# A rewritten head: load order, fold steps ahead of attention, and two batches hosted phase by phase

## The chip, the cores and the metric

The kernel runs on one core of a Trainium2 chip. The metric is the device time of one execution in microseconds (us), as the median of several runs. The engines named here are PE (matrix multiplications and transposes), ACT (exp and copies), DVE (products, reciprocals and copies), POOL (casts of loaded data) and SP (whose queue issues the loads). The program gives each engine its own list of instructions, and in the profile each works through its list in that order.

## What is computed

Eight batches of sparse causal attention, eight heads each, then a feed-forward network with a product in place of an activation:

```python
scores = scale * np.matmul(q, k.transpose(0, 1, 3, 2))       # 8 x 8 heads, 576 x 576, head size 64
mask_local = (rel >= 0) & (rel < stride)                      # heads 0 to 3
mask_strided = (rel >= 0) & (pos[None, :] % stride == pos[:, None] % stride)   # heads 4 to 7
...
x = np.ascontiguousarray(attn_out.transpose(0, 2, 1, 3)).reshape(B * S, H * D)   # 4608 x 512
a = x @ w1
b = x @ w2
h = a * b @ w3
return (h @ w_out).astype(np.float32)
```

The inner width d_ff is 1024. The kernel computes in fp16 with fp32 sums.

## The kernel before

**Tiling.** Since there is nothing between w3 and w_out, the kernel first forms their product w34 (the *fold*): eight blocks `jc`, each with eight transposes of w3 (`fold_tr`, tile `trp`, evacuated by one DVE and then one ACT copy into `w3T`) and eight matmuls in two halves (`fold_mm`, tile `ops`). The network then runs over nine tiles of 512 tokens. A tile has 24 *halves*, each of four 128x512 matmuls: sixteen of `ab_halves` (a: x by w1, copied out by ACT into `asb`; b: x by w2, multiplied with `asb` on DVE into `abt`) and eight of `o_halves` (o: `abt` by w34, copied out by ACT and stored).

**Attention** is done by pairs of heads, four pairs per batch, two local and then two strided. They are called P0 to P31 here; P0 to P3 are batch 0, P4 to P7 batch 1. The phases of a pair are:
- T: transposes of q and k into the PSUM tile `pt` (L224; for the first pair of a batch also those of the rest of the rows, L232), copied to `qT` and `kT` by ACT, or by ACT and DVE;
- S: scores (L266), into the tile `sps` and for the last columns into `pt`; then exp on ACT in two pieces (L286, `pte`) and the product with the mask on DVE (L287, `ptm`);
- PV: probabilities by v (L308), written into `sps` again, for strided pairs with a second part into the tile `pm`; then reciprocal and product on DVE (`rcp`, `xqs`, L312 and L313);
- T2: transposes back (L320), into the same buffer as `pm`, copied into `xT`, the input of the network.

There is one buffer each for `sps` (pool psA), for `pt` (psT) and for `pm` and T2 (psM). `ph_TS(s, t)` emits S of one pair and T of the next in one `pt` tile.

**Order.** All of PE's work is kept in the order in which it is written. A list `stream` holds the phases of all pairs with GAP marks between them (L407 to L447), and `host` emits the halves of a fold or a tile and, after each, the phases up to the next gaps, so that a tile's gaps are spread evenly over its halves. `batch_end[b]` is the place in the stream up to which a batch must be done before the next tile, because a tile needs the xT of its batch. Before, fold halves host batch 0; then the first nine or ten halves of tile 0 run without attention (`lead=9`), and the other halves of tile 0 host batch 1. From tile 1 on, tile t hosts batch t+1.

**Loads.** All loads are issued from SP's queue in written order, into nine staging buffers (`stg`), and cast to fp16, by POOL except for w1's four column blocks, which ACT casts. The order before is in the calls in front of the fold.

Of the kernel before, what the change touches and what calls it, by code (L numbers as in the profile page):

```python
# [19 lines left out]
def kernel(  # L20
# [12 lines left out]
    B, H, S, D = q.shape  # L33
# [7 lines left out]
    KF = DF // P  # L41
# [25 lines left out]
    AHEAD = 2  # L67

    def pe(ins):
        return tc.keep_in_program_order(ins)  # L70

    def copy(eng, out, in_):
        if eng == "a":
            nc.scalar.copy(out=out, in_=in_)  # L74
        elif eng == "v":
            nc.vector.tensor_copy(out=out, in_=in_)  # L76
        else:
            nc.gpsimd.tensor_copy(out=out, in_=in_)  # L78
# [47 lines left out]
    w1h = consts.tile([P, KM, DF], FP16)  # L126
    w2h = consts.tile([P, KM, DF], FP16)
# [9 lines left out]
    def load_wo(g, eng):  # L137
        src = moe_w_out.rearrange("(c p) n -> p c n", p=P)
        st = stgp.tile([P, 2, DM], FP32, tag="stg")
        nc.sync.dma_start(st, src[:, 2 * g:2 * g + 2, :])  # L140
        copy(eng, woh[:, 2 * g:2 * g + 2, :], st)

    def load_w3(jc, eng):
        st = stgp.tile([P, DF], FP32, tag="stg")
        nc.sync.dma_start(st, moe_w3[bass.ds(jc * P, P), :])
        t = ffn.tile([P, DF], FP16, tag="w3n", bufs=4)
        w3n[jc] = t
        copy(eng, t, st)

    def load_w12(g):  # L150
        cs = bass.ds(g * 256, 256)
        for wd, wh, eng in ((moe_w1, w1h, "a"), (moe_w2, w2h, "p")):
            st = stgp.tile([P, KM, 256], FP32, tag="stg")
            nc.sync.dma_start(st, wd.rearrange("(c p) n -> p c n", p=P)[:, :, cs])
            copy(eng, wh[:, :, cs], st)
# [4 lines left out]
    def load_qk(b, grp, engs="pp"):  # L160
        for nm, ten, eng in (("q", q, engs[0]), ("k", k, engs[1])):
            st = stgp.tile([P, 4, 4, D], FP32, tag="stg")
            nc.sync.dma_start(st.rearrange("p h c d -> p h (c d)"),
                              ten[b, 4 * grp:4 * grp + 4, 0:NM].rearrange("h (p c) d -> p h (c d)", c=4))
            t = qkp.tile([P, 4, 4, D], FP16, tag=f"{nm}{grp}")
            copy(eng, t, st.rearrange("p h c d -> p c h d"))
            x16[(b, nm, grp)] = t
# [20 lines left out]
    def load_vS(b):  # L188
        vt = v16S[b % 2]
        for hp in range(2):  # L190
            st = stgp.tile([SQ, 2, ST, D], FP32, tag="stg")
            sf = st.rearrange("p h c d -> p h (c d)")
            sv = v[b, 4 + 2 * hp:6 + 2 * hp].rearrange("h (p c) d -> p h (c d)", c=ST)
            nc.sync.dma_start(sf[0:64], sv[0:64])
            nc.sync.dma_start(sf[64:SQ], sv[64:SQ])
            nc.gpsimd.tensor_copy(out=vt[:, 2 * hp:2 * hp + 2, :, 0:D], in_=st)  # L196
# [5 lines left out]
    pairs = []  # L202
# [130 lines left out]
    def ab_halves(tch):  # L333
        tok = bass.ds(tch * NT, NT)
        res = []

        def first():
            abts[tch] = ffn.tile([P, KF, NT], FP16, tag="abt", bufs=4, name=f"abt{tch}")

        for jc in range(KF):  # L340
            st = {}

            def a(jc=jc, st=st):
                if jc == 0:
                    first()
                aps = psF.tile([P, NT], FP32, tag="f")
                for ci in range(KM):
                    pe(nc.tensor.matmul(aps, w1h[:, ci, bass.ds(jc * P, P)], xT[ci][:, tok],  # L348
                                        start=(ci == 0), stop=(ci == KM - 1)))
                asb = ffn.tile([P, NT], FP32, tag="asb")  # L350
                nc.scalar.copy(out=asb, in_=aps)  # L351
                st["asb"] = asb

            def bb(jc=jc, st=st):
                bps = psF.tile([P, NT], FP32, tag="f")
                for ci in range(KM):
                    pe(nc.tensor.matmul(bps, w2h[:, ci, bass.ds(jc * P, P)], xT[ci][:, tok],  # L357
                                        start=(ci == 0), stop=(ci == KM - 1)))
                nc.vector.tensor_mul(abts[tch][:, jc, :], bps, st["asb"])  # L359

            res += [a, bb]
        return res

    def acc_halves(lhs, rhs, done):
        st = {}

        def half(hf):
            if hf == 0:
                st["ps"] = psF.tile([P, NT], FP32, tag="f", name="ops")
            for ci in range(4 * hf, 4 * hf + 4):  # L370
                pe(nc.tensor.matmul(st["ps"], lhs(ci), rhs(ci), start=(ci == 0), stop=(ci == KF - 1)))  # L371
            if hf == 1:
                done(st["ps"])

        return [lambda: half(0), lambda: half(1)]

    def o_halves(tch):
        res = []
        for ts in range(NT // P):
            def done(ps, ts=ts):  # L380
                osb = ffn.tile([P, DM], FP32, tag="osb", bufs=3)
                nc.scalar.copy(out=osb, in_=ps)  # L382
                nc.scalar.dma_start(out_r[tch * (NT // P) + ts], osb)

            res += acc_halves(lambda ci, ts=ts: abts[tch][:, ci, bass.ds(ts * P, P)],
                              lambda ci: w34[:, ci, :], done)
        return res

    def fold_tr(jc):
        js = bass.ds(jc * P, P)  # L390
        ps = psF.tile([P, 1024], FP16, tag="f", name="trp")
        for kc in range(KF):
            pe(nc.tensor.transpose(ps[:, kc * P:(kc + 1) * P], w3n[jc][:, bass.ds(kc * P, P)], id16))
        pv = ps.rearrange("x (c j) -> x c j", j=P)
        nc.vector.tensor_copy(out=w3T[0][:, :, js], in_=pv[:, 0:4, :])
        nc.scalar.copy(out=w3T[1][:, :, js], in_=pv[:, 4:8, :])
# [10 lines left out]
    stream = []  # L407
    batch_end = {}

    def add(f, *a):  # L410
        stream.append(lambda: f(*a))

    GAP = object()

    def gaps(n):
        stream.extend([GAP] * n)
# [10 lines left out]

    for p, s in enumerate(pairs):
        b, i = divmod(p, 4)
        if i == 0 and b < AHEAD:  # L430
            add(ph_TS, None, s)
            gaps(2)
        t = pairs[p + 1] if p + 1 < len(pairs) else None
        if i == 3 and (b + 1 < AHEAD or b + 1 == B):
            t = None
        add(ph_TS, s, t)
        gaps(2)
        if i or b >= AHEAD:
            add(ph_T2, pairs[p - 1])
            if i == 0:  # L440
                batch_end[b - 1] = len(stream)
        gaps(1)
        add(ph_PV, s)
        gaps(3)
        if i == 3 and (b + 1 < AHEAD or b == B - 1):
            add(ph_T2, s)
            batch_end[b] = len(stream)  # L447
    pos = [0]

    def host(units, upto, lead=0):  # L450
        n = len(units) - lead
        total = sum(x is GAP for x in stream[pos[0]:upto])
        done = 0
        for i, u in enumerate(units):
            u()
            if i + 1 == len(units):
                tgt = total + 1
            else:
                tgt = (total * max(i + 1 - lead, 0)) // n
            while pos[0] < upto and done < tgt:  # L460
                x = stream[pos[0]]
                pos[0] += 1
                if x is GAP:
                    done += 1
                else:
                    x()
# [2 lines left out]
    load_w3(0, "p")  # L469
    for g in range(4):  # L470
        load_wo(g, "p")
    load_w3(1, "p")
    load_qk(0, 0)
    load_rest(0)
    load_w3(2, "p")
    load_vL(0)
    load_w3(3, "p")
    load_qk(0, 1)
    load_w3(4, "p")
    load_w3(5, "p")  # L480
    load_vS(0)
    load_w3(6, "p")
    load_w3(7, "p")
    load_w12(0)
    load_w12(1)
    load_w12(2)
    load_qk(1, 0)
    load_rest(1)
    load_w12(3)
    load_vL(1)  # L490
    load_qk(1, 1)
    load_vS(1)
# [1 line left out]
    fold = []  # L494
    fold_tr(0)
    for jc in range(KF):
        h0, h1 = fold_mm(jc)
        fold.append(h0)
        if jc + 1 < KF:
            fold.append(lambda jc=jc: fold_tr(jc + 1))  # L500
        fold.append(h1)
    host(fold, batch_end[0], lead=3)
    load_qk(2, 0)
    load_rest(2)
    load_vL(2)
    host(ab_halves(0), pos[0] + 11, lead=9)
    load_qk(2, 1)
    load_vS(2)
    host(o_halves(0), batch_end[1])
    for tch in range(1, NTILE):  # L510
        units = ab_halves(tch) + o_halves(tch)
        if tch + 1 < B:
# [45 lines left out]
```

## Time and profile before

| | us |
|---|---|
| median of three runs | 295.56 |
| lowest and highest | 294.17 and 297.71 |
| the profiled execution | 296.77 |
| its span, first to last instruction | 295.1 |
| PE busy / ACT / DVE / POOL in the span | 264.6 / 150.2 / 148.4 / 104.6 |
| S of P0, P1, P2, P3 | 23.74, 29.32, 34.93, 41.44 |
| first a of tile 0 | 48.0 |
| T of P4, S of P4 | 58.39, 60.88 |
| S of P5, P6, P7 | 66.26, 70.75, 76.40 |
| first a of tile 1 | 84.31 |

The times in the lower part are starts in the profiled execution, in us from the start of the span. A busy PE is not a PE at its peak: at full clock a half of four matmuls takes 0.86 us start to start, at the low granted clock 1.7 us. In the rows of the timeline the first number is the start, the second the time from the start to the end of the group, then engine, line, operation, output and input, the number of instructions, and in brackets the idle time of the engine before it with what ended it. "PEclk" or "granted clock" is the share of the TensorE clock that was granted.

### The profile page before, as it was taken

To read this page: it belongs to the slowest core of one execution; us is meant where nothing else is said; L and a number is where in the kernel's file an instruction comes from. 1 tells how busy PE (TensorE), PEld (TensorE's weight loads), DVE (VectorE), ACT (ScalarE), POOL (GpSimd) and SP (SyncE) were. 2 spreads that over 40 slices of the span, in tenths; PEclk is the share of its full clock that TensorE was granted. 3 is DMA by queue.
4 is the path that set the end of the run, shared out by engine and by line. 5 is a ranking of instruction groups with operands and counts; after the bars stand their busy time and mean duration, and the time that the engine had idled before them with its cause. 6 is when DMAs were issued, how large, how long until landed. Compare 5 with 4: busy or idle time off the path is not lost.

```text
span 295.1 us, 6686 instructions
## 1 busy us (share of the span) xinstructions
PE 264.6 (90%) x2689; PEld 135.8 (46%) x2689; DVE 148.4 (50%) x279; ACT 150.2 (51%) x309; POOL 104.6 (35%) x118
## 2 busy tenths in 40 slices
PE   2468987997779999999999999999999999999995
PEld 1133543444445554555455455545554554444442
DVE  2016563474556774765558567646654663330420
ACT  2025784467545556556565655555555655323332
POOL 5649644565445833557566424110000000000000
PEclk9988997999959999999999999999999999999999
DMA  7999999996879957997989892120011002103003
GB/s 247 346 219 344 302 347 264 216 265 122 270 233 224 253 106 206 264 180 243 259 172 286 177 273 49 36 109 3 0 73 74 0 2 107 38 0 138 4 3 142
DMA packets 58656, 48.68 MB, mean 165 GB/s; under 512 B 29184, under 2 KB 49664, under 8 KB 58624
## 3 DMA queue, kind: packets, MB, share of 16 engines
q1 hardware_dynamic: 53440, 38.81, 53.9%
q10 hardware_dynamic: 5184, 9.44, 8.9%
q8 instruction: 21, 0.34, 0.5%
q14 instruction: 11, 0.09, 0.1%
HBM read 38.80 MB, written 9.44 MB: 163 GB/s over the span
## 4 chain that ended last, share of the span: by engine, by line
PE 71%; ACT 10%; DMA 8%; DVE 5%; issue 3%; POOL 1%; SPq 1%
PE bps L357 21%; PE aps L348 20%; PE ops L371 17%; ACT pte L286 4%; PE sps L308 4%; DMA st<-in_moe_w_dram 3%; DMA st<-in_moe_w_out_dram 3%; PE sps L266 2%; DVE ptm L287 2%; PE ps L320 2%; ACT osb L382 2%; PE pt L224 2%; DVE xqs L313 1%; DMA out_dram<-osb 1%; PE pt L266 1%
## 5 line engine op out<-in xcount | busy, mean ns | idle before, releaser
L348 PE MATMUL aps<-xT,w1h 128*128 128x512 f16 x288 | 77.0, 386 | 3.6 <-ACT xT L327 3.6
L351 ACT COPY asb<-aps 128x512 f32<-128x512 f32 x72 | 43.0, 597 | 67.0 <-PE aps L348 65.3
L357 PE MATMUL bps<-xT,w2h 128*128 128x512 f16 x288 | 75.7, 386 | 0.0
L359 DVE TENSOR_TENSOR abt<-bps,asb 128x512 f16<-128x512 f32 x72 | 49.6, 689 | 50.1 <-PE bps L357 48.0
L371 PE MATMUL ops<-w,abt 128*128 128x512 f16 x288 | 68.5, 379 | 0.0
L78 POOL CAST t<-st 128x1024 f16<-128x1024 f32 (+1 forms) x48 | 48.2, 1011 | 32.7 <-DMA st<-in_k_dram 14.5
L357 PEld LDWEIGHTS <-w2h 128*128 128x128 f16 x288 | 26.9, 99 | 35.0 <-issue 7.7
L286 ACT ACTIVATE pte<-sps 128x960 f16<-128x960 f32 (+1 forms) x32 | 31.7, 990 | 19.1 <-PE sps L266 18.0
L348 PEld LDWEIGHTS <-w1h 128*128 128x128 f16 x288 | 26.7, 100 | 28.7 <-issue 1.9
L371 PEld LDWEIGHTS <-abt 128*128 128x128 f16 x288 | 25.9, 98 | 27.7
L185 POOL CAST v16L<-st 32x768 f16<-32x768 f32 (+1 forms) x32 | 27.9, 872 | 22.0 <-PE aps L348 7.6
L382 ACT COPY osb<-ops 128x512 f32<-128x512 f32 x36 | 21.5, 598 | 25.8 <-PE ops L371 25.8
L313 DVE TENSOR_TENSOR xqs<-sps,rcp 96x768 f16<-96x768 f32 (+1 forms) x32 | 32.6, 1018 | 0.7
L287 DVE TENSOR_TENSOR ptm<-pte,maskL 128x1152 f16<-128x1152 f16 x16 | 13.6, 852 | 28.7 <-ACT pte L286 28.7
L287 DVE TENSOR_TENSOR ptm<-pte,maskS 72x1152 f16<-72x1152 f16 x16 | 14.8, 928 | 25.6 <-ACT pte L286 25.6
L74 ACT COPY qT<-pt 128x256 f16<-128x256 f16 (+2 forms) x64 | 23.3, 410 | 7.7 <-PE pt L232 4.5
L196 POOL CAST v16S<-st 72x1024 f16<-72x1024 f32 x16 | 17.8, 1116 | 21.5 <-PE pm L308 11.6
L308 PEld LDWEIGHTS <-ptm 72*128 72x128 f16 (+1 forms) x448 | 18.2, 98 | 14.7 <-DVE ptm L287 7.1
L371 PE MATMUL ops<-woh,w3T 128*128 128x512 f16 x64 | 19.6, 438 | 2.1 <-POOL woh L78 1.2
L266 PEld LDWEIGHTS <-kT 64*128 64x128 f16 x448 | 10.1, 97 | 16.2 <-issue 10.6
L320 PEld LDWEIGHTS <-xqs 72*128 72x128 f16 (+1 forms) x224 | 12.0, 99 | 8.1 <-DVE xqs L313 1.6
L76 DVE COPY kT<-pt 128x128 f16<-128x128 f16 (+1 forms) x28 | 11.5, 435 | 7.5 <-ACT qT L74 7.5
(53 smaller groups left out, 201.1 us busy)
## 6 DMA issues: line engine op xcount, KB each, us to landing
out_dram<-osb ACTq DMA_DIRECT2D x36, 256.0 KB, 2.0
st<-in_moe_w_dram SPq DMA_DIRECT2D x16, 512.0 KB, 8.7
st<-in_q_dram SPq DMA_DIRECT2D x16, 512.0 KB, 5.3
st<-in_k_dram SPq DMA_DIRECT2D x16, 512.0 KB, 6.3
st<-in_v_dram SPq DMA_DIRECT2D x32, 144.0 KB, 7.1
st<-in_v_dram SPq DMA_DIRECT2D x16, 256.0 KB, 7.4
st<-in_moe_w_out_dram SPq DMA_DIRECT2D x4, 512.0 KB, 8.1
st<-in_q_dram SPq DMA_DIRECT2D x8, 128.0 KB, 7.8
```

The costliest lines, as they stand in the source:

```text
L78: nc.gpsimd.tensor_copy(out=out, in_=in_)
L185: nc.gpsimd.tensor_copy(out=vt[pr, hs, :, 0:D], in_=st[pr])
L286: nc.scalar.activation(out=pte[0:kr, lo:hi], in_=src, func=AF.Exp, bias=0.0, scale=scale)
L287: nc.vector.tensor_mul(ptm[0:kr, 0:2 * S].rearrange("p (a x) -> p a x", x=w), pte[0:kr].rearrange("p (a x) -> p a x", x=w), _ap(mk, 0, [[m ...
L308: pe(nc.tensor.matmul(xps[:, h, i * 65:i * 65 + 65], s.ptm[0:kr, c0:c0 + P], vt[0:kr, 2 * (s.hp % 2) + h, c, :], start=True, stop=True))
L313: nc.vector.tensor_mul(s.xqs[0:w, cs[0]:cs[0] + l].rearrange("p i h d -> p h i d"), xv[:, :, :, 0:D], _ap(rcp, 0, [[rcp.ap[0][0], w], [ST, ...
L348: pe(nc.tensor.matmul(aps, w1h[:, ci, bass.ds(jc * P, P)], xT[ci][:, tok], start=(ci == 0), stop=(ci == KM - 1)))
L351: nc.scalar.copy(out=asb, in_=aps)
L357: pe(nc.tensor.matmul(bps, w2h[:, ci, bass.ds(jc * P, P)], xT[ci][:, tok], start=(ci == 0), stop=(ci == KM - 1)))
L359: nc.vector.tensor_mul(abts[tch][:, jc, :], bps, st["asb"])
L371: pe(nc.tensor.matmul(st["ps"], lhs(ci), rhs(ci), start=(ci == 0), stop=(ci == KF - 1)))
L382: nc.scalar.copy(out=osb, in_=ps)
```

## The change

There are four edits.
1. w1's blocks are cast by POOL, as w2's.
2. The loads in front of the fold are reordered: w3's blocks 2 and 3 come ahead of batch 0's q and k, and w1 and w2's fourth block ahead of batch 1's first.
3. The stream: T of a batch's first pair is a phase of its own for batches 0 to 2; T of the second local pair's successor (P2 and P6) is split off into a phase of its own (`late`); T2 stands after one gap in place of two; batch 1 ends within its own tile, as batch 0 does.
4. Batches 0 and 1 are placed by hand: `run(units, plan)` reads a text in which "u" emits the next unit and a digit that many phases. The fold of blocks 0 to 2 runs ahead of the first T. All sixteen halves of a and b of tile 0 run without attention, and batch 1 lies among the eight o halves. `host` loses its `lead`.

```diff
-        for wd, wh, eng in ((moe_w1, w1h, "a"), (moe_w2, w2h, "p")):
+        for wd, wh, eng in ((moe_w1, w1h, "p"), (moe_w2, w2h, "p")):
...
         b, i = divmod(p, 4)
-        if i == 0 and b < AHEAD:
+        last = i == 3 and (b < AHEAD or b == B - 1)
+        if i == 0 and b <= AHEAD:
             add(ph_TS, None, s)
-            gaps(2)
+            gaps(1)
         t = pairs[p + 1] if p + 1 < len(pairs) else None
-        if i == 3 and (b + 1 < AHEAD or b + 1 == B):
+        late = b < AHEAD and i == 1
+        if late or (i == 3 and (b < AHEAD or b + 1 == B)):
             t = None
         add(ph_TS, s, t)
-        gaps(2)
-        if i or b >= AHEAD:
+        gaps(1)
+        if i or b > AHEAD:
             add(ph_T2, pairs[p - 1])
             if i == 0:
+                gaps(1)
                 batch_end[b - 1] = len(stream)
-        gaps(1)
+        if late:
+            add(ph_TS, None, pairs[p + 1])
+        gaps(1 if i == 0 and b > AHEAD else 2)
         add(ph_PV, s)
         gaps(3)
-        if i == 3 and (b + 1 < AHEAD or b == B - 1):
+        if last:
             add(ph_T2, s)
             batch_end[b] = len(stream)
...
+    def run(units, plan):
+        it = iter(units)
+        for ch in plan:
+            if ch == "u":
+                next(it)()
+            elif ch != " ":
+                step(int(ch))
...
-    load_w3(1, "p")
+    for jc in range(1, 4):
+        load_w3(jc, "p")
     load_qk(0, 0)
     load_rest(0)
-    load_w3(2, "p")
+    load_w3(4, "p")
     load_vL(0)
-    load_w3(3, "p")
     load_qk(0, 1)
-    load_w3(4, "p")
     load_w3(5, "p")
+    load_w3(6, "p")
     load_vS(0)
-    load_w3(6, "p")
     load_w3(7, "p")
     load_w12(0)
     load_w12(1)
     load_w12(2)
+    load_w12(3)
     load_qk(1, 0)
     load_rest(1)
-    load_w12(3)
...
-        fold.append(h0)
-        if jc + 1 < KF:
-            fold.append(lambda jc=jc: fold_tr(jc + 1))
-        fold.append(h1)
-    host(fold, batch_end[0], lead=3)
+        tr = [lambda jc=jc: fold_tr(jc + 1)] if jc + 1 < KF else []
+        fold += [h0] + tr + [h1] if jc < 4 else [h0, h1] + tr
+    run(fold, "uuuuuuuuu 1 uu 1 uu 1 u 3 u 1 u 1 uu 1 u 1 uu 1 u 1 u 2")
...
-    host(ab_halves(0), pos[0] + 11, lead=9)
+    for u in ab_halves(0):
+        u()
     load_qk(2, 1)
...
-    host(o_halves(0), batch_end[1])
+    run(o_halves(0), "u 1 u 1 uu 1 u 4 u 2 u 2 u 3")
```

On the engines this gives the following sequences on PE (halves a, b and o as above, tr the fold's transposes). Batch 1 before: T a b S T a b a PV b o S T o T2 PV o S T o T2 PV o o S T T2 o PV o, then S and T of the next pairs, T2, and tile 1. Batch 1 after: T o S T o o PV o S T2 T PV o S T T2 o PV S o T2 PV T2, and tile 1, which opens with a, T of P8, b, S of P8.

More of the change, by code (lines that the diff above doesn't have):

```diff
@@ L448, with step, host @@
     pos = [0]
-    def host(units, upto, lead=0):
-        n = len(units) - lead
+    def step(n):
+        while n:
+            x = stream[pos[0]]
+            pos[0] += 1
+            if x is not GAP:
+                x()
+                n -= 1
+    def run(units, plan):
[5 more added lines that the diff above has]
+                step(int(ch))
+        assert next(it, None) is None
+    def host(units, upto):
+        n = len(units)
         total = sum(x is GAP for x in stream[pos[0]:upto])
@@ L455, in host @@
             u()
[L456 to L459, printed above, removed]
+            tgt = total + 1 if i + 1 == n else total * (i + 1) // n
             while pos[0] < upto and done < tgt:
@@ L497 @@
         h0, h1 = fold_mm(jc)
-        fold.append(h0)
-        if jc + 1 < KF:
-            fold.append(lambda jc=jc: fold_tr(jc + 1))
-        fold.append(h1)
-    host(fold, batch_end[0], lead=3)
+        tr = [lambda jc=jc: fold_tr(jc + 1)] if jc + 1 < KF else []
+        fold += [h0] + tr + [h1] if jc < 4 else [h0, h1] + tr
+    run(fold, "uuuuuuuuu 1 uu 1 uu 1 u 3 u 1 u 1 uu 1 u 1 uu 1 u 1 u 2")
+    assert pos[0] == batch_end[0]
     load_qk(2, 0)
@@ L505 @@
     load_vL(2)
-    host(ab_halves(0), pos[0] + 11, lead=9)
+    for u in ab_halves(0):
+        u()
     load_qk(2, 1)
     load_vS(2)
-    host(o_halves(0), batch_end[1])
+    run(o_halves(0), "u 1 u 1 uu 1 u 4 u 2 u 2 u 3")
+    assert pos[0] == batch_end[1]
     for tch in range(1, NTILE):
```

## The prediction, made before the changed kernel had run

> **What bounds the kernel now.** First the page, for shares and the forty slices.
>
> ```profile
> PE 264.6 (90%) x2689; PEld 135.8 (46%) x2689; DVE 148.4 (50%) x279; ACT 150.2 (51%) x309; POOL 104.6 (35%) x118
> PE   2468987997779999999999999999999999999995
> DMA  7999999996879957997989892120011002103003
> ```
>
> Past slice 12 (89 us) PE shows 9 in every slice until the tail, so nothing but PE time counts there. What can change lies in the first 89 us. There DMA is full for the first 57 us and PE is not, so I cut the head into the 3.41 us steps in which the granted clock changes. Columns: busy us of PE, granted clock, DMA share, GB/s.
>
> ```profile
> 17.22:20.63 3.41, 1.00 (x26) 1.00 1.33 174
> 20.63:24.05 3.42, 2.98 (x22) 0.50 1.04 313
> 44.53:47.94 3.41, 1.76 (x27) 1.00 1.20 260
> 47.94:51.35 3.41, 3.41 (x15) 0.50 1.13 256
> 71.83:75.25 3.42, 2.13 (x29) 1.00 0.69 134
> 78.66:82.07 3.41, 1.52 (x20) 1.00 0.48 162
> 82.07:85.49 3.42, 2.67 (x39) 0.50 0.76 214
> 85.49:88.90 3.41, 3.41 (x19) 0.50 1.10 308
> ```
>
> After a step in which PE was busy for 1.76 us or less, the next step runs at half clock; after 2.13 us it does not. A low step full of matmuls loses up to 1.7 us.
>
> Then the timeline, for what the attention waits for. One turn of it, pair P5 to P6:
>
> ```profile
> 66.43 0.39 PE L266 MATMUL sps<-qT,kT 64*128 64x96 f16 x10
> 66.86 0.97 ACT L286 ACTIVATE pte<-sps 128x960 f16<-128x960 f32 x1 [2.00 <-PE sps L266]
> 67.72 0.33 ACT L286 ACTIVATE pte<-pt 128x192 f16<-128x192 f32 x1
> 68.08 0.76 DVE L287 TENSOR_TENSOR ptm<-pte,maskL 128x1152 f16<-128x1152 f16 x1 [1.11 <-ACT pte L286]
> 68.90 0.54 PE L308 MATMUL sps<-v16L,ptm 128*128 128x65 f16 x12 [0.58 <-DVE ptm L287]
> 69.74 0.95 DVE L313 TENSOR_TENSOR xqs<-sps,rcp 96x768 f16<-96x768 f32 x1
> 70.75 0.40 PE L266 MATMUL sps<-qT,kT 64*128 64x72 f16 x14 [0.31 <-DVE xqs L313]
> ```
>
> PV writes into the score tile and there is one such tile, so the next S waits until xqs is read out: S to S was 4.5 us (66.26 to 70.75) with PE idle inside. Other turns took 5.4 to 6.5 us because halves or copies stood in the way. A turn holds about 2 us of attention on PE, so it needs some three halves of 0.86 us to fill it. Last, the ends of the tiles and the port hit:
>
> ```profile
> PE aps L348 <- ACT xT L327: 3.6, 6, 0.7
> 36.97 1.04 POOL L78 CAST t<-st 128x1024 f16<-128x1024 f32 x1 [0.30 <-DMA st<-in_moe_w_dram]
> 37.00 1.61 DVE L287 TENSOR_TENSOR ptm<-pte,maskS 72x1152 f16<-72x1152 f16 x1 [1.14 <-ACT pte L286]
> ```
>
> A mask product beside a POOL cast took 1.61 us, alone 0.76.
>
> **Part 1: loads, fold, batch 0.** No matmul, DMA or byte is added or removed. Two more w3 loads of 0.5 MB go ahead of q and k; such loads land 1.34 to 1.54 us apart (casts at 10.95, 12.29, 13.83), so q, k and rest come 2.9 us later and the cast of rest goes from 18.25 to 21.15. T of P0 ends at 21.8 and its copies, as in 18.92 to 21.12, at 24.0. Ahead of S0 the changed instruction order has one o half and the fold transposes of w3 block 4, whose cast follows rest by 1.7 us and takes 1.04 (23.9); transposes at the low clock take 1.0 us. So S0 is at 24.7, against 23.74. The fold steps done earlier (two halves and two sets of transposes, about 3 us) come out of DMA waiting and cost nothing, but the turns that they leave are not bound by PE. Turn by turn, in the changed order of ACT and DVE:
> - P0: ACT's copy of the fold stands ahead of exp (to 25.8), exp 1.2, mask 1.32 beside the v casts as in the row at 25.56, a v copy of 0.33 to 1.05 now between mask and PV, PV 0.54, xqs 1.2: S1 at 30.8 (6.1; before 5.57).
> - P1: T of P2 is a phase by itself now and needs the one pt tile, which exp of P1 reads until 1.95 after S1; then fold transposes, PV, xqs: 4.9, S2 at 35.7 (before 5.61).
> - P2: two halves, transposes and T2 stand ahead of PV; its second part waits for ACT's xT copy, queued behind exp, four copies of P3's T and two of the fold: 6.8, S3 at 42.5 (before 6.5).
> - P3: fold copy on ACT ahead of exp (0.9 late), then as before less the w1 cast of 0.93 that stood between its two exps: T2 at 48.6, against 47.70.
> Term: +0.9. Bounds: if every turn took its least (S0 23.9, then 4.5, 4.5, 5.0 and 5.3, the last from 41.43 to 47.70 less the cast), T2 at 43.2, -4.5; if the w1 casts, now POOL's (four of 1.04 us, beside w2's), hit the last mask, +0.6 more. I take +0.9, since the copies that I count stand in the order in every turn. SP's queue: w12's fourth column block passes q, k and rest of batch 1, so it comes at about 50 in place of 55; nobody needs it before half 13 (59). Batch 1's loads come 3 us later, with their use 6 us later.
>
> **Part 2: tile 0 and batch 1.** Before, ten halves ran bare from 48.0, then T of P4 at 58.39, and fourteen halves lay among the four pairs. Now sixteen and one run bare: 48.0 + 1.7 (low clock) + 17 x 0.864 = 64.4 for T of P4, and seven halves (6.0 us) are left for four turns. PE's work in them, 6.0 and 7.2 of attention (four S of 0.45, three T and four T2 of 0.43, PVs of 0.55 and 0.65), is far under their length. By rows: T to S 2.5 (58.39 to 60.88), 66.9; two turns of 4.5, 75.9; a strided one of 4.75 (exp 1.3, mask 0.76, PV 0.6, xqs 1.4, S 0.45, hand-overs 0.25), 80.6; last S to T2's end 5.5 (41.43 to 47.70 less the cast, plus 0.1), 86.1. Before, T2 of P7 ended at 84.3, with S of P8 and T of P9 done. Now tile 1's first a waits for xT (0.7), runs cold (to 87.3), T of P8 0.8, b 1.7 (89.8), and S of P8 waits: its four copies alternate between ACT and DVE on one tile (0.6, 0.68, 0.45, 0.42), and abt's product (0.69, ready only after b) stands ahead of the last on DVE: 91.0. S and T 0.8, PV 0.55: 92.35. The same work was done at 88.73 before. Term: +3.6. Turns shorter than 4.5, which no row shows, would be needed to take from it; POOL hits and the xT wait (row 70.75 to 76.41: 5.66) would add up to 2.
>
> Low steps: PE's share in 64.4 to 86.1 is 13.2 / 21.7, or 2.1 us per step, nearest to the 2.13 that kept the clock. I take 0 and keep +3.4 (two steps) and, were the end warm, -1.7.
> The Trainium skill, page "TensorE: Matmul & The Clock Gate", section "HAM oscillation — how this bites in real kernels", gives as its rule that only PE idle gaps over some 3.4 us matter. The rows differ: the longest gap in 44.53:47.94 was 1.5 us (before the PV at 45.46), and the next step was low. By the page the +3.4 cannot come, and the rival that needs it, below, would keep 0.05.
>
> **Part 3: T2 one unit earlier.** The changed order shows it inside every batch: S, T, b, T2, a, b, PV. At the tile ends it is unchanged from tile 2 on (S, T, o, T2, a), as the last unit takes all that is left. So the 3.6 us of waits stay. At the end of tile 1 it is worse: 27 gaps for 24 halves put S, T and T2 all behind the last o. xT, queued behind exp and qT, comes 3.25 after S; PE has 1.7 of work: wait 1.5, against 0.84 before (113.99 to 114.83): +0.7. PV's waits for xT (0.6 in all past 88 us) may go: -0.4.
>
> **Sum.** 0.9 + 3.6 + 0.7 - 0.4 = +4.8 on the profiled 296.77 (span 295.1 and 1.7 outside), 301.6. The median of the three runs is 295.56, 1.2 less: 300.4.
>
> **Rivals.**
> - *Short turns in batch 0, warm ends: faster.* If the fold copies slip between the exps and turns take 4.5 to 5.0, T2 of P3 comes at 43.2; the idle step before 47.9 goes, and with it a low step. Sum: -4.5 - 1.7 + 3.6 + 0.3 = -2.3, and with a warm tile 1 -4.0: 291.5. It decides where S3 starts before 38. For it: ACT has four casts of 1.0 less. Against: the fold copies stand in ACT's order ahead of two exps. 0.12.
> - *Half of that: no change.* T2 of P3 at 45 to 46 with batch 1 as forecast: 296 to 298. 0.22.
> - *More cold steps and hits.* Turns in batch 1 that slip under 1.76 us per step, doubling T, S, PV: +8, 304. 0.11.
> - *The change does what its words say.* T2 a half earlier at six ends saves 6 x 0.84 = 5.0: 295.4. The instruction order speaks against it; its chance is within the 0.22.
> - The forecast, 300.4: 0.55.
>
> **Numbers.** This kernel's measurement tells about 1% (3 us) from no change. Slower 0.55 + 0.11 = 0.66, same 0.22, faster 0.12. The range goes from 294 (part of batch 0's gain, most of the no-change case) to 305 (two cold steps).
>
> **What would show it.** T of P4 at 63 to 66, S of P4 to P7 4.5 to 5 apart with PE idle inside, tile 1's first a at 85 to 88, a wait near 1.5 us at tile 2's first a. T2 of P3 before 45, or tile 1 before 83, makes the forecast wrong; so would batch 1 at under 4.4 us a turn.

## The result, and the profile after

The changed kernel took 306.06 us in the median of four runs (304.47 to 307.76), the kernel before 295.31 (294.17 to 297.71): a ratio of 1.0354, 95% interval 1.0262 to 1.0445. That is 10.75 us more, where 4.8 were forecast, and above the forecast range. Ratios here leave out executions that lie more than 1.5% above the fastest of their kernel; since some kernels below spread wider than that, a table after the experiments has the mean of all executions as well.

| start, us from the start of the span | before | after | later by |
|---|---|---|---|
| S of P0 | 23.74 | 26.72 | 3.0 |
| T2 of P3 | 47.71 | 51.36 | 3.7 |
| first a of tile 0 | 48.01 | 51.62 | 3.6 |
| T2 of P7 | 83.84 | 90.90 | 7.1 |
| PE goes on behind PV of P8 and tile 1's first five halves | 91.40 | 102.16 | 10.8 |
| first a of tile 2 | 113.34 | 124.04 | 10.7 |
| first a of tile 8 | 270.67 | 281.64 | 11.0 |
| end of the span | 295.1 | 306.0 | 10.9 |

The whole loss has arisen by the end of PV of P8 and of the first five halves of tile 1; tiles 2 to 8 take as long as they did (157.60 us from first a to first a, before 157.33). The page of the changed kernel, its busy times and its slices:

```profile
PE 268.6 (88%) x2689; PEld 137.8 (45%) x2689; DVE 150.1 (49%) x279; ACT 147.3 (48%) x305; POOL 107.1 (35%) x122
PE   2295886996668999899999999999999999999995
PEclk9999699899965999999999999999999999999999
DMA  7998999794688992899899974021003002102003
```

PE has as many instructions as before and is busy 4.0 us longer, which is work done at the low clock. In the clock's line the 6 at the fifth slice (31 to 38 us) is new, and the 6 and 5 at the twelfth and thirteenth (84 to 99 us) stand where before there was one 5. The table by clock steps shows the stretch; columns are busy us of PE, PEld, DVE, ACT and POOL (instructions), granted clock, DMA share, GB/s.

```profile
69.74:73.15 3.41, 1.55 (x34) 0.96 (x34) 1.28 (x3) 1.48 (x5) 1.66 (x2) 1.00 0.35 43
83.39:86.80 3.41, 1.97 (x35) 1.31 (x36) 1.98 (x5) 1.54 (x4) 2.02 (x2) 1.00 0.27 62
86.80:90.21 3.41, 2.15 (x26) 1.54 (x24) 2.01 (x5) 1.74 (x4) 0.48 (x1) 0.50 1.08 279
90.21:93.63 3.42, 2.73 (x30) 1.35 (x32) 0.95 (x3) 0.97 (x2) 2.98 (x4) 0.50 1.07 330
93.63:97.04 3.41, 2.30 (x24) 0.75 (x20) 1.71 (x4) 1.28 (x4) 1.74 (x2) 0.50 0.49 127
97.04:100.45 3.41, 3.41 (x34) 1.71 (x35) 1.36 (x2) 2.23 (x4) 1.23 (x2) 0.50 1.22 208
```

Four steps in a row are at half clock around the opening of tile 1, where before there were two. The first turn of batch 1 in the timeline:

```profile
70.34 0.23 DVE L76 COPY kT<-pt 128x128 f16<-128x128 f16 x1 [1.23 <-ACT qT L74]
70.48 0.95 DVE L186 COPY v16L<-v16L 32x640 f16<-32x640 f16 x1
70.82 1.85 ACTq L383 DMA_DIRECT2D out_dram<-osb  x1
71.35 0.27 DVE L76 COPY kT<-pt 128x128 f16<-128x128 f16 x1
71.68 0.42 PE L266 MATMUL sps<-qT,kT 64*128 64x96 f16 x10
72.72 0.97 ACT L286 ACTIVATE pte<-sps 128x960 f16<-128x960 f32 x1 [1.93 <-PE pt L224]
73.94 0.76 DVE L287 TENSOR_TENSOR ptm<-pte,maskL 128x1152 f16<-128x1152 f16 x1 [2.33 <-ACT pte L286]
74.76 0.54 PE L308 MATMUL sps<-v16L,ptm 128*128 128x65 f16 x12 [0.59 <-DVE ptm L287]
76.61 0.39 PE L266 MATMUL sps<-qT,kT 64*128 64x96 f16 x10 [0.30 <-DVE xqs L313]
```

A copy of v stands between the two copies of kT on DVE, so T to S takes 3.35 us (T of P4 starts at 68.32), before 2.49. And the store of tile 0's first o half is issued by ACT at 70.82, ahead of P4's exp: the issue holds ACT for 1.85 us, and exp, whose scores are complete at about 72.1, begins at 72.72, 0.05 us after the issue ends and 0.6 after the scores. The bracket gives ACT's idle time to PE; what ended last is seen only in the row of the issue. Before, the first store was issued at 69.66, between the exps of P5 and P6. The group of all 36 stores (duration in ns: least, median, most; first and last start), of the kernel before:

```profile
L383 ACTq DMA_DIRECT2D out_dram<-osb x36: 338/338/374, 69.7 to 292.2; - x36
```

and of the kernel after:

```profile
L383 ACTq DMA_DIRECT2D out_dram<-osb x36: 338/338/1849, 70.8 to 303.2; - x36
```

Last, the end of tile 1, in the waits and in the timeline of the kernel after:

```profile
PE aps L348 <- ACT xT L327: 4.1, 6, 1.2
```

```profile
124.04 0.81 PE L348 MATMUL aps<-xT,w1h 128*128 128x512 f16 x3
126.03 0.38 PE L348 MATMUL aps<-xT,w1h 128*128 128x512 f16 x1 [1.18 <-ACT xT L327]
```

### The profile page after: what moved, and what is told of

Same layout as the page of the kernel before. It is cut to its first block, busy times and chain, and to the rows that moved or that the text cites. A ratio compares the mean times of both kernels' runs of the same rounds, so it can differ in the third digit from the quotient of the medians.

```text
span 306.0 us, 6690 instructions
## 1 busy us (share of the span) xinstructions
PE 268.6 (88%) x2689; PEld 137.8 (45%) x2689; DVE 150.1 (49%) x279; ACT 147.3 (48%) x305; POOL 107.1 (35%) x122
## 4 chain that ended last, share of the span: by engine, by line
PE 70%; ACT 9%; DVE 8%; DMA 7%; issue 3%; SPq 1%; ACTq 1%; POOL 0%; POOLq 0%
PE bps L357 20%; PE aps L348 19%; PE ops L371 19%; DMA st<-in_moe_w_dram 7%; PE sps L308 4%; ACT pte L286 4%; DVE ptm L287 3%; DVE xqs L313 2%; PE sps L266 2%; PE pt L224 2%; PE ps L320 2%; ACT osb L382 2%; ACT xT L327 1%; PE pt L266 1%; ACT qT L74 1%
## 5 line engine op out<-in xcount | busy, mean ns | idle before, releaser
L185 POOL CAST v16L<-st 32x768 f16<-32x768 f32 (+1 forms) x32 | 27.0, 845 | 28.4 <-PE bps L357 9.1
L287 DVE TENSOR_TENSOR ptm<-pte,maskS 72x1152 f16<-72x1152 f16 x16 | 13.9, 869 | 26.2 <-ACT pte L286 26.2
L196 POOL CAST v16S<-st 72x1024 f16<-72x1024 f32 x16 | 16.6, 1049 | 15.2 <-PE pm L308 7.6
L266 PEld LDWEIGHTS <-kT 64*128 64x128 f16 x448 | 10.4, 97 | 19.1 <-issue 11.4
L320 PE MATMUL ps<-id,xqs 72*128 72x72 f16 (+1 forms) x224 | 14.3, 207 | 3.2 <-DVE xqs L313 3.2
## 6 DMA issues: line engine op xcount, KB each, us to landing
st<-in_moe_w_dram SPq DMA_DIRECT2D x16, 512.0 KB, 10.4
```

The lines of the kernel that those rows point to most:

```text
L287: nc.vector.tensor_mul(ptm[0:kr, 0:2 * S].rearrange("p (a x) -> p a x", x=w), pte[0:kr].rearrange("p (a x) -> p a x", x=w), _ap(mk, 0, [[m ...
L320: pe(nc.tensor.transpose(ps[:, t * w:(t + 1) * w], s.xqs[0:w, t].rearrange("p h d -> p (h d)"), id16[0:w, 0:w]))
```

## The experiments

"Low time" below is 2 x (1 - mean granted clock) x span, the time at half clock in one execution. Each edit is against the kernel named. Where "fillers" are named, extra matmuls into a tile that nobody reads were added at places where PE idles, to keep its clock; in a plan the letters a, b, c and d stand for two, four, six and eight of them.

**1. The loads alone (e1_loads).** The kernel before with the new load order and w1 cast by POOL.

```diff
-    load_w3(1, "p")
+    for jc in range(1, 4):
+        load_w3(jc, "p")
     load_qk(0, 0)
...
-        for wd, wh, eng in ((moe_w1, w1h, "a"), (moe_w2, w2h, "p")):
+        for wd, wh, eng in ((moe_w1, w1h, "p"), (moe_w2, w2h, "p")):
```

> The kernel before with the changed load order and w1's casts on POOL, nothing else. Theory L (the late data of the load order are what batch 0 loses): first a of tile 0 about 3 us later than 48.0, time 3 to 3.7 above before. Theory H (the hosting by hand loses it, the loads cost only what rest lands later, some 1.5 us): +0.5 to +2. Theory P (POOL's casts beside the mask): ptm of P3 over 1.3 us, +0.6.

293.58 us in the median of 10 against 295.03; ratio 0.9964 (0.9921 to 1.0006). S of P0 came at 24.25. The later q and k and the casts on POOL together cost nothing that can be measured; tile 0 began at 47.70.

**2. Batch 1 as before (e2_undo_b1).** The changed kernel with batch 1 spread over a, b and o halves of tile 0 as before.

```diff
-    for u in ab_halves(0):
-        u()
+    run(ab_halves(0), "uuuuuuuuuu 1 uu 1 uuu 1 u")
...
-    run(o_halves(0), "u 1 u 1 uu 1 u 4 u 2 u 2 u 3")
+    run(o_halves(0), "u 1 u 3 u 1 u 2 uu 1 u 2 u 1")
```

> The changed kernel, but tile 0 hosts batch 1 as before: ten halves bare, then T of P4, six halves a and b and the eight o among the pairs. Theory A (turns of batch 1 too short of halves): first a of tile 1 comes 3 to 4 us earlier than 91.4, and with fewer half-clock steps after it the time is 4 to 6 below the changed kernel (300 to 302). Theory T (tile 1's opening with T and S of P8 is what costs): 0 to 2 below.

298.43 (295.59 to 299.41, 4 runs); ratio 1.0118 (1.0043 to 1.0194). About two thirds of the loss is in the place of batch 1. The store's place goes with it: here it is issued between the exps of later pairs, in 0.38 us.

**3. Tile 1's opening as before (e3_undo_T8).** The changed kernel, with T of P8 again beside S of P7, and S of P8 with T of P9 again ahead of tile 1.

```diff
-        last = i == 3 and (b < AHEAD or b == B - 1)
-        if i == 0 and b <= AHEAD:
+        last = i == 3 and (b + 1 < AHEAD or b == B - 1)
+        if i == 0 and b < AHEAD:
...
-        if late or (i == 3 and (b < AHEAD or b + 1 == B)):
+        if late or (i == 3 and (b + 1 < AHEAD or b + 1 == B)):
...
-        if i or b > AHEAD:
+        if i or b >= AHEAD:
...
-                gaps(1)
+                gaps(1 if b > AHEAD else 0)
...
-    run(o_halves(0), "u 1 u 1 uu 1 u 4 u 2 u 2 u 3")
+    run(o_halves(0), "u 1 u 1 uu 1 u 4 u 2 u 2 u 4")
```

> The changed kernel, but T of P8 goes with S of P7 and S of P8 with T of P9 ahead of tile 1, as before. Theory T (the opening of tile 1): 2.5 to 3.7 below the changed kernel, with tile 1's a and b back to back. Theory A: 1 or less below, since the end of batch 1 stays late and cold.

303.63 (298.95 to 306.07, 4 runs); ratio 1.0208 (1.0102 to 1.0314), which rests on two of the four executions; the spread of 7 us leaves it open. Its first store took 3.19 us to issue, at 63.18.

**4. A warm clock in batch 1 (e4_warm).** The changed kernel with 26 fillers (its expectation counts 22) among the o halves of tile 0.

```diff
+    def fill(n):
+        fps = psF.tile([P, NT], FP32, tag="f", name="fps")
+        for _ in range(n):
+            pe(nc.tensor.matmul(fps, w1h[:, 0, 0:P], w2h[:, 0, 0:NT], start=True, stop=True))
...
+            elif ch in "abcd":
+                fill(2 * "abcd".index(ch) + 2)
...
-    run(o_halves(0), "u 1 u 1 uu 1 u 4 u 2 u 2 u 3")
+    run(o_halves(0), "u 1 ub 1 uu 1 u 2b2 u 2 ub 1b1 u 1b1c 1")
```

> The changed kernel with 22 filler matmuls, read by nobody, in batch 1's idle places on PE. Theory C (half-clock steps are the cost): granted clock 1.0 up to tile 1's opening, 3 to 5 below the changed kernel. Theory A (latency of the turns): turns stay 4.3 to 4.9, first a of tile 1 within 1 us of 91.4; only the half clock after it can be saved, 0 to 3 below.

302.03 (301.44 to 303.61, 4 runs); ratio 1.025 (1.0183 to 1.0317). The clock stayed up past 54.5 us; the steps around tile 1's opening (89.19) in this kernel:

```profile
85.16:88.58 3.42, 3.14 (x35) 1.49 (x33) 2.99 (x5) 1.35 (x4) 1.49 (x2) 1.00 0.96 240
88.58:91.99 3.41, 2.88 (x40) 1.28 (x40) 1.13 (x4) 1.71 (x3) 1.90 (x3) 1.00 0.98 328
91.99:95.40 3.41, 2.00 (x35) 1.24 (x36) 1.64 (x5) 1.97 (x5) 1.82 (x2) 1.00 0.64 145
```

Its low time, 7.8 us in the mean, is no more than that of the kernel before on the same chip (8.6). So the clock can be a part of the loss, and more than half is something else, to which any time that the fillers themselves cost would be added.

**5. Part 1 alone (e5_b0_only).** The edits of 2 and 3 together, with the last plan as "u 1 u 3 u 1 u 2 uu 2 u 1 u 2": loads, fold, batch 0 and the split T of P6 are changed, batch 1's place and tile 1's opening are as before.

> The changed kernel with its loads and its batch 0, but batch 1 among six halves a and b and the eight o, and S of P8 with T of P9 ahead of tile 1, as before: both undone that gave 4.0 and 3.7 us from tile 0 to tile 2 one by one. Theory A with T (the two add up): 7 to 8 below the changed kernel, first a of tile 0 to first a of tile 2 at 63 to 66. If batch 0's own plan loses (first a of tile 0 at 49 to 52), time stays at 297 to 299; if what the first profile showed there was the clock, 47 to 48 and 293 to 296.

297.32 against 295.68 (10 and 19 runs); ratio 1.0044 (1.0007 to 1.008): +1.3 us, 0.2 to 2.4.

**6. A warm clock in batch 0 (e6_warm_b0).** The changed kernel with twelve fillers (its expectation counts ten) in batch 0.

```diff
-    run(fold, "uuuuuuuuu 1 uu 1 uu 1 u 3 u 1 u 1 uu 1 u 1 uu 1 u 1 u 2")
+    run(fold, "uuuuuuuuu 1 uu 1 uud 1 u 2b1 u 1 u 1 uu 1 u 1 uu 1 u 1 u 2")
```

> The changed kernel with ten filler matmuls ahead of PV of P0 and ahead of T of P2, nothing else. Theory C0 (the 3.6 us of batch 0 are the two half-clock steps at 32 to 39, which start where PE waits for PV of P0): no low step before 45, first a of tile 0 at 46 to 48.5, 2 to 4 below the changed kernel. Theory Q (its queues of copies): 50 to 52, no gain.

303.74 (303.27 to 306.87, 4 runs); ratio 1.0294 (1.0229 to 1.036). Tile 0 began at 47.9 in place of 51.6, but little of that arrived: the first store took 2.59 us, and batch 1 had three low steps (71.5 to 75, 85.2 to 92).

**7. T2 earlier at the tile ends (e7_t2_early).** The kernel before, with what the words of the change say and its order of instructions does not do from tile 2 on: T2 of a batch's last pair one half ahead of the tile's end.

```diff
-        gaps(2)
+        end = i == 0 and b >= AHEAD
+        gaps(1 if end else 2)
         if i or b >= AHEAD:
             add(ph_T2, pairs[p - 1])
             if i == 0:
+                gaps(2)
                 batch_end[b - 1] = len(stream)
-        gaps(1)
+        gaps(0 if end else 1)
```

> The kernel before with one edit: T2 of a batch's last pair stands one half ahead of the last unit of the tile in place of behind it, so that a half lies between T2 and the next tile's first a. By the 0.84 us that each of six tile ends waits for xT: 4 to 5 below before (290 to 291). If ACT's queue only moves the wait: 0 to 1 below.

292.94 against 295.68 (10 and 19 runs); ratio 0.9914 (0.9874 to 0.9953). The waits of this kernel (total, times, longest):

```profile
PE pm L308 <- ACT xT L327: 2.6, 5, 0.7
PE pm L308 <- DVE xT L76: 1.5, 5, 0.3
PE pm L308 <- ACT xT L74: 0.2, 1, 0.2
PE aps L348 <- ACT xT L327: 1.3, 2, 1.0
```

The 3.6 us of waits for xT at the tile ends fell to 1.3, but PV's second part, which needs the buffer of T2, now waits 4.3 us inside the tiles, where it waited 0.9.

**8. The changed kernel again (e8_again).** No edit; for a second profile.

> The changed kernel once more, unedited, for the spread of its head. If the 51.6 us to the first a of tile 0 were chance in part, it comes at 46 to 50 here, by how many half-clock steps fall before it.

305.49 (303.77 to 306.62, 4 runs); ratio 1.0336 (1.0266 to 1.0405). In this execution batch 0 was fast, tile 0 began at 45.18, and yet tile 1 at 89.57. The first turn of batch 1, in the timeline:

```profile
64.38 4.40 ACTq L383 DMA_DIRECT2D out_dram<-osb  x1
64.61 0.42 PE L266 MATMUL sps<-qT,kT 64*128 64x96 f16 x10
65.20 1.90 PE L371 MATMUL ops<-w,abt 128*128 128x512 f16 x8
68.83 0.97 ACT L286 ACTIVATE pte<-sps 128x960 f16<-128x960 f32 x1 [4.48 <-issue]
70.06 0.76 DVE L287 TENSOR_TENSOR ptm<-pte,maskL 128x1152 f16<-128x1152 f16 x1 [5.51 <-ACT pte L286]
70.88 0.84 PE L308 MATMUL sps<-v16L,ptm 128*128 128x65 f16 x12 [3.78 <-DVE ptm L287]
```

The same store took 4.40 us to issue; exp began 3.80 us after its scores were complete, mask and PV came behind it, and PE stood still for 3.78 us. Half-clock steps followed from 70.0 to 80.3. S of P4 to S of P5 took 8.75 us. What batch 0 had gained was gone. This row was the first view of a cause that no theory had named.

**9. The first store from SP's queue (e9_store_sp).** The changed kernel; on SP the store stands behind loads and is issued at 82.5.

```diff
-                nc.scalar.dma_start(out_r[tch * (NT // P) + ts], osb)
+                (nc.scalar if tch or ts else nc.sync).dma_start(out_r[tch * (NT // P) + ts], osb)
```

> The changed kernel, but the first output store of tile 0 is issued from SP's queue, behind batch 2's loads, in place of ACT's, where it stood ahead of P4's exp and took 1.85, 3.19, 4.40, 1.57 and 2.59 us to issue in five profiles. Theory St (the issue holds ACT while the loads fill the DMA queues): S of P4 to its PV 3.1 us in place of 3.1 to 6.3, median 1 to 3 below the changed kernel, most in executions whose batch 0 ends early. Rival (the load itself is what P4 waits for): S to PV as long as before, time unchanged.

300.91 (298.6 to 303.09, 4 runs); ratio 1.0214 (1.0122 to 1.0306). The first turn of batch 1:

```profile
65.63 0.60 PE L266 MATMUL sps<-qT,kT 64*128 64x96 f16 x10
66.27 0.97 ACT L286 ACTIVATE pte<-sps 128x960 f16<-128x960 f32 x1 [1.61 <-PE sps L266]
66.59 3.14 PE L371 MATMUL ops<-w,abt 128*128 128x512 f16 x8
69.57 0.53 PE L308 MATMUL sps<-v16L,ptm 128*128 128x65 f16 x12
```

Exp of P4 now starts 0.04 us after its scores are there. S to PV takes 3.9 us, against 6.3 in experiment 8 but 3.1 in the first profile: here the two halves between S and PV ran at half clock (3.14 us).

**10 to 12. Combinations.** e10_store_T8: edits 3 and 9. e11_all3: edits 3, 4 and 9 (the plan ends in "1b1c 2"). e12_best: the kernel before with the loads of 1 and T2 one gap earlier inside the batches as well as at the ends, with two gaps between T2 and PV.

```diff
-        gaps(2)
+        end = i == 0 and b >= AHEAD
+        gaps(1 if end or b >= AHEAD else 2)
...
+                gaps(2)
                 batch_end[b - 1] = len(stream)
-        gaps(1)
+        gaps(0 if end else 2 if b >= AHEAD else 1)
```

> That edit and T, S of P8 ahead of tile 1 as before. If the two add: 4.5 to 6 below the changed kernel, 299.5 to 301. If undoing the opening of tile 1 was the same gain under another name: 302 to 304, as with it alone.

> Both edits and the filler matmuls in batch 1. If clock, store and tile 1's opening are all that batch 1 loses against before: 295 to 297. If the turns themselves lose time with seven halves in them: first a of tile 0 to first a of tile 2 stays 2 us or more above the 62.7 to 65.5 of the kernels that host batch 1 as before, time 297.5 to 300.

> The kernel before with the changed loads (w1 on POOL), T2 one half ahead of the last unit at the tile ends, and T2 one half earlier inside the batches. By the sum of what they gave alone (1.4 and 2.7) and of the PV waits for xT that came with the second (2.6 + 1.2 us): 288.5 to 291. If those waits stay: 291 to 292.

e10: 300.5 (298.86 to 304.39), ratio 1.0207 (1.0119 to 1.0296). e11: 300.72 (297.06 to 302.04), 1.0249 (1.0154 to 1.0343). Neither came near the kernel before, though e11 undoes all three of the suspected costs. e10 lies where the sum of two gains was expected, but experiment 9 alone had come as far. In e11's profile tile 0 and tile 1 together took 68.5 us with 3.4 of them at half clock; in experiments 1 and 7, which have batch 1 where it was and the same 3.4, they took 62.7 and 62.8. (The ratio of e11 is above what its four executions give in the mean, +4.9 us or 1.017; the table below has the mean.) e12: 287.2 (285.16 to 289.51), ratio 0.975 (0.9662 to 0.9838), the fastest of all, 8.0 +- 3.1 us ahead of the kernel before in the mean, and ahead of the 288.5 to 291 that were expected. Of that, tiles 2 to 8 account for 4.4 us in the profiles (152.9 us, before 157.3). Its waits of xT:

```profile
PE pm L308 <- ACT xT L74: 0.9, 2, 0.7
PE aps L348 <- ACT xT L327: 0.3, 1, 0.3
```

With two gaps behind T2, both waits are small at once, which experiment 7 had not reached.

**13 and 14. The missing corners.** e13_store_warm: the changed kernel with edits 4 and 9. e14_warm_T8: with edits 3 and 4.

> The changed kernel with the first store on SP's queue and the fillers in batch 1; tile 1 opens as in the changed kernel. If the store's issue and the half clock are two costs that add (4.6 to 5 and 3.8 by the medians so far): 297 to 299. If they are one cost seen twice (the store's stall makes the idle step, and the step the half clock): 300 to 302, as with each alone.

> The fillers and T, S of P8 ahead of tile 1, with the first store on ACT's queue: the kernel with all three edits but the store. If the store's issue costs time by itself: 2 to 4 above that kernel, with S of P4 to its PV over 4 us wherever the first a of tile 0 comes before 47. If the fillers hide it: the same within 1 us.

e13: 298.88 (296.62 to 301.49, 6 runs), ratio 1.0103 (1.0036 to 1.017). e14: 302.95 (300.24 to 304.85, 6 runs), 1.0231 (1.0166 to 1.0296). e13 came where two costs that add were expected; e14 and e11 differ by 2 us, which is within the interval of e11. With that there are all eight combinations of three edits to the changed kernel. Means of all executions, less the mean of the kernel before on the same chip, with 95% intervals of the two means:

| first store on | fillers | tile 1's opening | us against before | mean low time, us |
|---|---|---|---|---|
| ACT | no | changed | +9.8 (two sets, +-1.5) | 22.2 |
| ACT | no | as before | +8.3 +- 4.9 | 13.5 |
| ACT | yes | changed | +7.5 +- 1.5 | 7.8 |
| ACT | yes | as before | +7.0 +- 1.8 | 10.4 |
| SP | no | changed | +5.6 +- 3.1 | 14.2 |
| SP | no | as before | +5.8 +- 3.7 | 14.7 |
| SP | yes | as before | +4.9 +- 3.7 | 8.1 |
| SP | yes | changed | +3.3 +- 2.0 | 4.4 |

The kernel before had 8 to 11 us of low time on the same chips. The store makes -4.2, -4.2, -2.4 and -2.1 in the four pairs of rows that differ in it alone, -3.2 +- 2.2 in the mean; the interval counts that three of the rows with SP lean on one set of seven executions of the kernel before. With the executions alone that the ratios use, the pairs are -3.9, -4.6, +0.1 and -2.5, in the mean -2.7 +- 1.9. The fillers make -2.3, -2.3, -1.2 and -0.9, in the mean -1.7 +- 1.6: all of one sign, and at the edge of what can be told from zero. Tile 1's opening makes -1.5, +0.2, -0.5 and +1.6: nothing that can be seen. A fifth pair has batch 1 where it was: experiment 5 less experiment 2, -2.2 +- 2.5. What the opening costs stays open.

## Why the prediction was wrong

**Part 1, +0.9: right.** Experiment 5 measured +1.3 (0.2 to 2.4), and the loads alone -1.1 (-2.3 to +0.2). The turns came near to what was worked out in experiment 5's profile, where S of P0 to P3 start at 24.75, 30.81, 35.45 and 41.42 (forecast 24.7, 30.8, 35.7 and 42.5); in experiment 8's, S of P3 came 3.6 earlier than forecast. The 3.6 us by which tile 0 starts later in the changed kernel's profile are not typical: ten other executions with this batch 0 started tile 0 between 45.18 and 51.04, half of them before 47.6. In that profile PV of P0 waited for the mask and for a v copy, and two low steps (32.2 to 39.0) followed; twelve fillers there took those steps away, and hardly any time.

**Part 2, +3.6: two of its terms failed.** The turns themselves came near in the first profile: S of P4 to P7 stood 4.9, 4.3 and 4.9 us apart (forecast 4.5 to 4.75), and tile 1's first a followed 5.6 after the last S (forecast 5.5 up to T2's end; the 47.70 that this rests on is T2's start, 0.3 before its end). But the chain from T of P4 did not run as written:
- **The store ahead of exp, put at nothing.** The seven o halves were counted as PE time that fills the turns, and what each brings onto ACT, a copy and a DMA issue ahead of exp, was not counted. This is the largest miss that an experiment shows: -3.2 +- 2.2 us when that one store leaves ACT. In the six profiles in which it stood on ACT ahead of P4's exp, the issue was 1.57 to 4.40 us long, and exp began 0.6, 0.6, 0.6, 2.0, 2.3 and 3.8 us after its scores were complete; in the ten others, 0.04.
- **"T to S 2.5"** was taken from a place where no v copy stood between the copies of kT. It is 2.49 in all six profiles with batch 1 as before, and 2.7 to 3.4 in the ten with a v copy there.
- **"I take 0"** for low steps, since PE's share, 2.1 us per step, was near to that of a step that kept the clock. That was a mean: single steps of batch 1 in the first profile had 1.55 to 2.57, and the one with 1.97 at its end lost the clock. The eight executions of the changed kernel had 17 to 27 us of low time, in the mean 22.2, against 9 in the kernel before. Part of that comes from the store: with it on SP, 14.2 are left. Fillers leave 7.8, and bring some 1.7 us; with both, 4.4.
- The opening of tile 1, costed within the +3.6 as S of P8 waiting for its copies, could not be told from nothing when undone.

With store and clock both mended, two rows of the table are left: +4.9 +- 3.7 and +3.3 +- 2.0, in the mean 4.1 +- 2.0, which holds the forecast sum of 4.8. Less some 1 of Part 1, about 3 remain for turns and opening, where 3.6 had been put. So this part of the forecast's mechanism is not contradicted, though the sum in the first profile below shows that its terms were not all near. What was missing, about 5 to 6 us, is by these experiments the store's issue and the steps at half clock. How the two share it is known only to within some 2 us each. An estimate from the slope in the last section, 0.27 us for each us at half clock, gives 3.6 us for 13 us more of low time, which is within what the fillers show.

One profile can differ from that mean. In the first one the excess over the forecast at PV of P8, 6.3 us, was 2.7 from batch 0, 0.3 from the bare halves, 0.85 from T to S, 0.4 from the three turns (the store's 0.6 lies in them), 0.1 up to T2's end, 0.7 up to S of P8, and 1.3 from the three halves behind it, with half clock up to 100.5.

**Part 3, +0.3: right.** The waits at tile ends were 3.6 and are 4.1 us, all six still there; at the end of tile 1 the wait before the fourth matmul went from 0.68 to 1.18 and PV's waits for xT past 88 us from 0.6 to 0.3. Of its two terms, the +0.7 measured +0.5 and the -0.4 measured -0.3. That the words of the change promise more than its order does is shown by experiments 7 and 12, where the move is made at all ends and pays.

**The rivals.** "More cold steps and hits" named 304 and was the nearest, for half of the reason: the clock, but not POOL, as the four mask products of batch 1 took 0.75 to 0.89 us. "Short turns in batch 0, warm ends" had its condition nearly met in experiment 8 (S of P3 at 38.89, where it asked for 38; tile 0 at 45.18) and would still have been wrong: where batch 0 ends earlier, the store's issue is longer, and the turn of P4 gives the gain back. Issued ahead of 67 us it took 2.6 to 4.4 us (experiments 3, 6 and 8), from 69 on 1.6 to 1.9. This may also be why filling batch 0 gained next to nothing.

**The clock rule.** By the Trainium skill, page "TensorE: Matmul & The Clock Gate", section "HAM oscillation — how this bites in real kernels", only idle gaps of PE over some 3.4 us cost the clock. The gap of 3.78 us in experiment 8 agrees. The four low steps from 86.80 of the changed kernel do not: the longest gap in the step ahead of them was 1.02 us, before S of P7 at 85.79.

## What to carry to other kernels

When work is moved ahead of a chain that is bound by latency, count on every engine what the moved work issues, its DMA issues above all: a store on the queue of the engine that computes exp is part of that engine's chain. A loop that waits on such a chain needs enough matmuls in each turn for the clock as well as for the time; here seven halves in four turns went with 22 us at half clock. And an order written as gaps should be read as the instructions come out: T2 one half earlier, together with the new load order, gained 8 us once it truly stood there and its buffer's next user stood two gaps behind it.

## What the runs showed of the hardware

**An issue that holds its engine.** On ACT a store's issue took 0.34 to 0.43 us nearly everywhere, 0.63 to 0.83 once near 200 us in four profiles, and 1.57 to 4.40 us in one place, ahead of P4's exp. Loads on SP's queue are often as long, 29 of 132 over 0.8 us in the kernel before, and there nobody's exp stands behind them; one of them in the same stretch:

```profile
64.48 2.93 SPq L183 DMA_DIRECT2D st<-in_v_dram  x1
```

The Trainium skill, page "Perfetto Trace Analysis", section "DMA Instruction — HWDGE (DVE, Sync)", says that the profiled time of an issue includes waiting for a descriptor generator that several queues share. In the changed kernel no issue of SP is on record between 66.8 and 77.6 us, so waiting for another's issue is not what these rows show. Nor is it the load of the DMA engines alone: in experiment 2 the store was issued in 0.38 us, at 68.54, at a DMA share of 1.29, and in experiment 14 it took 1.68 us at a share of 0.03 and less. Nor does it last until the DMA engines are idle: in the last 0.85 us of the issue their share was 0.05 or less in five profiles, but 0.96 in experiment 3. What holds it stays open.

**No plain threshold for the clock.** By the rows of before, a step with PE busy for 1.76 us or less was followed by half clock, and one with 2.13 was not. In the changed kernel a step with 1.55 (69.74) kept the clock, and one with 1.97 (83.39) lost it. In the profiles of the two kernels full clock came back after steps with 2.98 or more, and not after 2.80 or less. Executions of one kernel differ with the number of such steps: 50 executions of the kernel before lie between 291.8 and 299.3 us, and their time rises by 0.27 us for each us at half clock (correlation 0.73, which is about half of their variance).
